# Splitting an expert's weights only where the expert changes, for slots 2 to 4 of a mixture of experts

## The chip, the cores and the metric

The kernel runs on one core of a Trainium2 chip, in one launch. The metric is device time in microseconds; lower is better. A core has five engines that run beside each other and wait for each other by semaphores: TensorE (PE in the profile, its weight loads as PEld), VectorE (DVE), ScalarE (ACT), GpSimd (POOL) and SyncE (SP), which here only issues transfers.

## The reference, cut to what matters

Three layers follow each other; all arrays are float32 (`w_in` and `w_out` are drawn as float32 too, the kernel is handed them as float64 bits).

```python
# 1. attention: 4 batches x 8 heads, 576 tokens, head size 64, with a decay by f, causal
scores = where(causal, -1e9, q @ k.T / 8 + cum[:, None] - cum[None, :]);  x = softmax(scores) @ v
# 2. mixture of experts, one expert per token: 2304 tokens, D = 512, 8 experts, F = 1024
e_idx = argmax(x @ w_gate + modality_bias[modality_id]);  gate = softmax(...)[e_idx]
for e in range(8):
    mask = e_idx == e
    out[mask] = gate[mask] * (relu(x[mask] @ w1[e]) @ w2[e])
# 3. feed-forward: 512 -> 2048 -> 512
h = x @ w_in;  y = maximum(0.01 * h, h) @ w_out
```

## The kernel before, in words

**Precision.** A float32 product is made of three matmuls of a faster 32-bit format: a matrix is split in a high half (a cast, done by ScalarE) and a low half (matrix less high half, by VectorE), and high x high, low x high and high x low are summed in PSUM. Activations and weights are split so, on the chip.

**Attention** (to about 232 us) runs over 16 pairs of heads. Its last pieces overlap with the first of the experts. While it runs, the tokens are routed: `route(b)` per batch finds each token's expert and its place among that expert's tokens. After three of four batches `route1` already lays out the first `K1 = 4` *slots*: a slot is 128 tokens of one expert, and the first slots are filled with the experts' full groups of 128, in the order of the experts. `ef` is the expert of each slot, `nw` is 1 where it differs from the slot before (always 1 for slot 0), `ei` and `ni` are these as integers. `finish` lays out the other slots once all batches are routed; its first part and the rest of `route(3)` are written ahead of the slots' loop, outside of any fixed order, so the planner puts their instructions between others.

**Experts.** `step(t)` runs for each slot: the first 18 always, up to 7 more under nested conditions (`rest`), and `tail` ends it. Step t does slot t's first product and, one step late, slot t-1's second. In the order of TensorE: `gemm1(t)` for k 0 and 1 (12 matmuls of 512 columns), `trh(t-1)` (8 transposes of slot t-1's hidden layer, split in `hh` and `hl`), `gemm1(t)` for k 2 and 3, `gemm2(t-1)` for k 0 to 3, `trx(t+1)` (4 transposes of the next tokens, split in `xh` and `xl`), `gemm2(t-1)` for k 4 to 7; in step 0 and for t < 3 `trh` and `trx` stand a little elsewhere. `keep(t)`, on ScalarE, takes `gemm1`'s result through the relu to `hs`; `yout(t)` scales the second product by the gate and scatters it.

The weights of an expert are 4 + 4 tiles of 128 x 1024. `load(t, which, k)` brings one of them (512 KB) into `w1r[k]` or `w2r[k]`; from slot 1 on the transfer has a condition, a register made from `ni`, and is not carried out where the expert is the same. `split(t, which, k)` then makes `w1h[k]`, `w1l[k]` (or `w2h`, `w2l`) of it with one ScalarE cast and one VectorE subtraction, for every slot, and issues the load of slot t+1 into the tile that has come free. There is one set of raw and of split tiles. `split(t+1, 0, k)` stands in step t, each k where `gemm1(t)` is done with that tile; `split(t, 1, k)` stands in step t, k 0 and 1 behind the first half of `gemm2(t-1)`, k 2 and 3 at the end of the step.

**Order.** `with ordered(tc, MS2)` fixes the order of all five engines as it is written in the steps; what is written outside is placed by a planner that simulates the times. A conditional block (`tc.If`) is a piece of its own: nothing is put between its instructions. Beside the experts, the first weights of the third layer are loaded and converted in small pieces (`wpart`, `aside`). **The third layer** follows from about 499 us on, in the planner's order.

```python
nc.scalar.copy(hi[k], raw[k])
nc.vector.tensor_tensor(lo[k], raw[k], hi[k].bitcast(F32), ALU.subtract)
if t + 1 < NS:
    load(t + 1, which, k)
```

Of the kernel before, what the change touches and what calls it, by code (L numbers as in the profile page):

```python
# [9 lines left out]
F32 = mybir.dt.float32  # L10
F32R = mybir.dt.float32r
BF16 = mybir.dt.bfloat16
I32 = mybir.dt.int32
AF = mybir.ActivationFunctionType
ALU = mybir.AluOpType
AX = mybir.AxisListType
# [3 lines left out]
P = 128  # L20
# [11 lines left out]
NS = NSTAT + E - 1  # L32
# [5 lines left out]
K1 = 4  # L38
# [35 lines left out]
def fused(ctx: ExitStack, tc, qk0, qk2, vp, f, mid, wg, mb, w1, w2, w_in, w_out, out):  # L74
    nc = tc.nc
    w_in = w_in.bitcast(I32)
    w_out = w_out.bitcast(I32)
    cp = ctx.enter_context(tc.tile_pool(name="const", bufs=1))
# [43 lines left out]

    gidx, oidx, ei, ni = ([cp.tile([P, n] + d, I32, name=f"{c}{n}") for n in (K1, N2)] for c, d in (("gidx", []), ("oidx", [2]), ("ei", []), ("ni", [])))
    nt = cp.tile([P, 1], I32, name="nt")

    mr = ExitStack()
    rt = mr.enter_context(tc.tile_pool(name="rt", bufs=1, side="right"))
# [13 lines left out]
    with tc.tile_pool(name="pst", bufs=PST, space=PSUM) as pst:  # L141
# [48 lines left out]
        def load(g):  # L190
            if g == 1:

                xt[0] = pe.tile([P, NC, XW], F32, tag="x", name="x0")
                raw = xt[0].rearrange("p c d -> p (c d)")[:, :2 * S].rearrange("p (h s) -> p h s", h=2)
            else:
                raw = pe.tile([P, 2, S], F32, tag="raw", name=f"raw{g}", bufs=3)
            nc.sync.dma_start(raw, qk2[:, 2 * g:2 * g + 2, :])
            ops[g] = raw
# [234 lines left out]
        def xout(g):  # L433
            b, gg = divmod(g, H // 2)
            if gg == 0 and b:
                xt[b] = (pe, pre)[b % 2].tile([P, NC, XW], F32, tag="x", name=f"x{b}")
            x = xt[b]
            lp = lps[b % 2]
            rr = a3.tile([P, NC, 2], F32, tag="rr", name=f"rr{g}")

            nc.vector.tensor_copy(sms[g % 3][:64, 4, 1:2], sms[g % 3][64:, 4, 0:1])
            nc.vector.tensor_scalar(rr, sms[g % 3], 1e-9, None, ALU.add)
            nc.vector.reciprocal(rr, rr)
            for part, c0, n in ((0, 0, 3), (1, 3, 2)):
                xu = st.pop((g, "x", part))
                ps = pst.tile([P, 512], F32, tag="t", name=f"xo{g}_{part}")
                for i in range(n):
                    nc.tensor.matmul(ps[:, i * HW:(i + 1) * HW], lhsT=xu[:, i * P:(i + 1) * P], rhs=idw[:, gg, :], start=True, stop=True)
                i0 = ps[:, :n * HW].rearrange("p (c d) -> p c d", d=HW)
                sc = rr[:, c0:c0 + n, :].unsqueeze(3)  # L450
                for o, a, w in ((x[:, c0:c0 + n, gg * P:(gg + 1) * P], slice(0, P), D), (lp[:, c0:c0 + n, gg, :], slice(P, HW), E)):
                    nc.vector.tensor_tensor(o.rearrange("p c (j d) -> p c j d", j=2), i0[:, :, a].rearrange("p c (j d) -> p c j d", j=2), sc.to_broadcast([P, n, 2, w]), ALU.mult)
            if gg == H // 2 - 1:
                routing.append(route(b))
                if b == B - 2:
                    routing.append(route1(pre, (B - 1) * NC))
# [77 lines left out]
        def scan(a, n):  # L534
            t = [rt.tile([P, 4 + E], F32, name=f"scan{n}{i}") for i in range(2)]
            for i in t:
                nc.vector.memset(i, 0.0)
            nc.vector.tensor_copy(t[0][:, 4:], a)
            for s in (1, 2, 4):
                nc.vector.tensor_add(t[1][:, 4:], t[0][:, 4:], t[0][:, 4 - s:4 + E - s])  # L540
                t = t[::-1]
            inc = t[0][:, 4:]
            exc = rt.tile([P, E], F32, name=f"exc{n}")
            nc.vector.tensor_sub(exc, inc, a)
            return inc, exc

        def slots(tp, n, inc):
            s3 = [P, n, E]
            gi = tp.tile(s3, F32, name=f"gi{n}")
            nc.vector.tensor_tensor(gi, slott[:, :n].unsqueeze(2).to_broadcast(s3), inc.unsqueeze(1).to_broadcast(s3), ALU.is_ge)  # L550
            ef = rt.tile([P, n], F32, name=f"ef{n}")
            nc.vector.tensor_reduce(ef, gi, axis=AX.X, op=ALU.add)
            return gi, ef

        def per_token(tp, name, a, m):
            s2 = [P, m, E]
            u = tp.tile(s2, F32, tag="u", name=f"u{name}")
            nc.vector.tensor_tensor(u, oall[:, :m], a.unsqueeze(1).to_broadcast(s2), ALU.mult)
            o = tp.tile([P, m], F32, name=name)
            nc.vector.tensor_reduce(o, u, axis=AX.X, op=ALU.add)  # L560
            return o


        def table(tp, n, m, stk, pool, tag, h2p):
            s4 = [P, m, n]
            h1 = tp.tile(s4, BF16, name=f"h1{n}")
            nc.vector.tensor_tensor(h1, slott[:, :n].unsqueeze(1).to_broadcast(s4), stk.unsqueeze(2).to_broadcast(s4), ALU.is_equal)
            h2 = h2p((m, 2, n))
            for i in range(2):
                nc.vector.tensor_tensor(h2[:, :, i, :], h1, idf[:, i, :m].unsqueeze(2).to_broadcast(s4), ALU.mult)  # L570
            yield
            ps = pool.tile([P, 512], F32, tag=tag, name=f"tp{n}")
            for i in range(m):
                r = rows_of(i % NC)
                nc.tensor.matmul(ps[:, :2 * n], lhsT=lall[:r, i, :], rhs=h2[:r, i].rearrange("p a t -> p (a t)"), start=(i == 0), stop=(i == m - 1))
            tq = tp.tile([P, 2 * n], F32, name=f"tq{n}")
            nc.vector.tensor_copy(tq, ps[:, :2 * n])
            idt = rt.tile([P, n], F32, name=f"idt{n}")
            nc.vector.scalar_tensor_tensor(idt, tq[:, :n], 64.0, tq[:, n:], ALU.mult, ALU.add)
            nc.vector.tensor_scalar(gidx[n == N2], idt, -1.0, 0.0, ALU.add, ALU.max)  # L580
            yield idt
# [4 lines left out]
        def route1(tp, m):  # L586
            fi = tp.tile([P, E], I32, name="fi")
            full = rt.tile([P, E], F32, name="full")
            nc.vector.tensor_copy(fi, runb)
            nc.vector.tensor_scalar(fi, fi, 7, None, ALU.logical_shift_right)  # L590
            nc.vector.tensor_copy(full, fi)
            yield
            inc, exc = scan(full, 1)
            yield
            used = rt.tile([P, E], F32, name="used")
            nc.vector.tensor_scalar(used, exc, -1.0, float(K1), ALU.mult, ALU.add)
            nc.vector.tensor_scalar(used, used, 0.0, None, ALU.max)
            nc.vector.tensor_tensor(used, used, full, ALU.min)
            yield
            gi, ef = slots(rt, K1, inc)  # L600
            nw = tp.tile([P, K1], F32, name="nw1")
            nc.vector.memset(nw, 1.0)
            nc.vector.tensor_tensor(nw[:, 1:], ef[:, 1:], ef[:, :K1 - 1], ALU.not_equal)
            nc.vector.tensor_scalar(ei[0], ef, float(E - 1), None, ALU.min)
            nc.vector.tensor_copy(ni[0], nw)
            yield
            stk = per_token(tp, "stk1", exc, m)
            yield
            lim = per_token(tp, "lim1", full, m)
            yield  # L610
            nc.vector.tensor_tensor(lim, jall[:, :m], lim, ALU.is_ge)
            nc.vector.scalar_tensor_tensor(stk, lim, BIG, stk, ALU.mult, ALU.add)
            nc.vector.tensor_add(stk, stk, jall[:, :m])
            yield
            for _ in table(tp, K1, m, stk, pst, "t", lambda d: tp.tile([P, *d], BF16, name="h2")):
                for _ in range(T1):
                    yield
            early.update(full=full, used=used, gi=gi, ef=ef)
# [170 lines left out]
    with tc.tile_pool(name="rt2", reuse_waits="tile", bufs=1) as rt2, \  # L789
# [40 lines left out]
            nc.gpsimd.indirect_dma_start(out=xg[t % 2], out_offset=None, in_=xs[:n, :], in_offset=bass.IndirectOffsetOnAxis(ap=m[:, i:i + 1], axis=0), bounds_check=n - 1, oob_is_err=False)  # L830

        def split(t, which, k):
            raw, hi, lo = (w2r, w2h, w2l) if which else (w1r, w1h, w1l)
            nc.scalar.copy(hi[k], raw[k])  # L834
            nc.vector.tensor_tensor(lo[k], raw[k], hi[k].bitcast(F32), ALU.subtract)  # L835
            if t + 1 < NS:
                load(t + 1, which, k)

        def trx(t):
            ps = pmx.tile([P, 512], F32, tag="tx", name=f"tx{t}")  # L840
# [57 lines left out]
        def tail(t):  # L898
            with ordered(tc, MS4):
                trh(t)  # L900
                ps = [(pmx, "tx"), (pm0, "th"), (pm1, "th")]
                xtr(0, xp0, ps, [0])
                split(t, 1, 2)
                split(t, 1, 3)
                gemm2(t, 0, 4)
                xtr(0, xp0, ps, [1, 2, 3])
                gemm2(t, 4, NFB)
                yout(t)
# [5 lines left out]
        def step(t):  # L914
            nx = t + 1 < NS
            if not t:
                split(t, 1, 0)
                split(t, 1, 1)
# [260 lines left out]
```

## Time and profile before

| | |
|---|---|
| time, median of 3 runs | 914.2 us (913.07 to 915.13) |
| profiled execution, its own time | 911.09 us |
| its span, first to last instruction | 909.4 us |
| TensorE busy | 863.0 us (95%) |
| VectorE busy | 629.2 us (69%) |
| ScalarE busy | 526.4 us (58%) |
| GpSimd busy | 141.9 us (16%) |
| one weight split | 1054 or 1051 ns on ScalarE, 1221 or 1217 on VectorE |
| weight splits | 84 of w1, 80 of w2 (20 slots ran) |

The page also cuts the span in 40 slices of 22.7 us, a digit for the busy tenths of each:

```profile
PE   5999899898979999999999999999999999999995
DVE  6677768588899999999987364368336943473333
ACT  5877767577768899999986353354223422232221
PEclk9999999999999999999999999999999999999998
```

The experts lie in slices 11 to 22. An engine's idle time costs something only where another, in the end TensorE, waits for it; which wait that is, is read from the timeline. PEclk is the clock granted to TensorE.

### The profile page before, as it was taken

How to read it: one execution, taken by the hardware profiler on the slowest of the kernel's cores; microseconds unless marked ns; L12 is line 12 of the kernel's file. 1: busy time of each engine (PE TensorE's matmuls, PEld its weight loads, DVE VectorE, ACT ScalarE, POOL GpSimd, SP SyncE). 2: the span in 40 equal slices, each digit the busy share in tenths (PEclk: the TensorE clock that was granted, in tenths of full speed). 3: DMA queues.
4: the chain of work that ended last, by engine and by line, in shares of the span. 5: the costliest groups of instructions: out<-in, count | busy, mean ns of one | idle time of the engine just before them, and what ended most of it. 6: DMA issues, size and time to landing. Idle time of an engine off the chain costs nothing. (4 is left out here: it accounts for less than half of the span.)

```text
span 909.4 us, 14373 instructions
## 1 busy us (share of the span) xinstructions
PE 863.0 (95%) x4733; PEld 710.0 (78%) x4733; DVE 629.2 (69%) x1091; ACT 526.4 (58%) x993; POOL 141.9 (16%) x181
## 2 busy tenths in 40 slices
PE   5999899898979999999999999999999999999995
PEld 3877777776758788888877888888888888888885
DVE  6677768588899999999987364368336943473333
ACT  5877767577768899999986353354223422232221
POOL 5000000000112324454532100000000000001112
PEclk9999999999999999999999999999999999999998
DMA  5776867758338516422231232024000400011111
GB/s 154 221 175 166 210 162 176 200 120 276 74 98 281 155 42 188 132 70 70 84 103 38 83 94 81 1 70 114 2 1 25 136 27 0 1 47 47 47 47 69
DMA packets 32962, 92.91 MB, mean 102 GB/s; under 512 B 7317, under 2 KB 7989, under 8 KB 32882
## 3 DMA queue, kind: packets, MB, share of 16 engines
q1 hardware_dynamic: 28082, 76.71, 29.6%
q0 software_dynamic: 4800, 15.23, 5.3%
q8 instruction: 39, 0.64, 0.3%
q14 instruction: 41, 0.34, 0.1%
HBM read 132.09 MB, written 14.99 MB: 162 GB/s over the span
## 5 line engine op out<-in xcount | busy, mean ns | idle before, releaser
L1085 DVE SCALAR_TENSOR_TENSOR us<-u,us 128x512 f32<-128x512 f32 (+1 forms) x80 | 51.0, 637 | 126.2 <-ACT us L1084 125.6
L1084 ACT COPY us<-u 128x512 f32<-128x512 f32 (+1 forms) x80 | 43.5, 544 | 162.8 <-PE u L1082 162.7
L1082 PE MATMUL u<-fxl,whii 128*128 128x512 f32 (+1 forms) x320 | 118.1, 369 | 0.0
L1082 PE MATMUL u<-fxh,wloi 128*128 128x512 f32 (+1 forms) x320 | 117.9, 368 | 0.0
L1082 PE MATMUL u<-fxh,whii 128*128 128x512 f32 (+1 forms) x320 | 116.8, 369 | 0.7 <-ACT fxh L740 0.7
L1102 PE MATMUL a<-whio,gh 128*128 128x512 f32 x288 | 112.8, 392 | 0.0
L1102 PE MATMUL a<-wloo,gh 128*128 128x512 f32 x288 | 112.3, 390 | 0.0
L1102 PE MATMUL a<-whio,gl 128*128 128x512 f32 x288 | 106.0, 390 | 0.0
L835 DVE TENSOR_TENSOR w1l<-w1r,w1h 128x1024 fp32r<-128x1024 f32 x84 | 100.8, 1221 | 4.6 <-ACT w1h L834 4.1
L835 DVE TENSOR_TENSOR w2l<-w2r,w2h 128x1024 fp32r<-128x1024 f32 x80 | 94.4, 1217 | 0.9 <-ACT w2h L834 0.7
L834 ACT CAST w1h<-w1r 128x1024 fp32r<-128x1024 f32 x84 | 85.8, 1054 | 2.3 <-PE h L854 2.2
L339 ACT ACTIVATE p<-sc,nm 128x128 f32<-128x128 f32 (+3 forms) x128 | 66.1, 526 | 31.3 <-DVE nm L334 28.4
L834 ACT CAST w2h<-w2r 128x1024 fp32r<-128x1024 f32 x80 | 81.4, 1051 | 2.8 <-PE y L882 2.2
L1088 ACT CAST gh<-us 128x512 fp32r<-128x512 f32 (+1 forms) x80 | 46.2, 578 | 58.7 <-DVE us L1085 39.4
L1089 DVE TENSOR_TENSOR gl<-us,gh 128x512 fp32r<-128x512 f32 (+1 forms) x80 | 50.9, 636 | 39.8 <-ACT gh L1088 39.0
L334 DVE TENSOR_REDUCE nm<-sc 128x2 f32<-128x256 f32 (+1 forms) x64 | 51.1, 819 | 30.0 <-PE sc L328 22.5
L882 PE MATMUL y<-w2h,hl 128*128 128x512 f32 x160 | 64.0, 400 | 5.5 <-DVE hl L875 5.4
L1112 POOL DMA_INDIRECT out<-acc,tid x18 | 17.9, 995 | 327.2 <-DVE acc L1109 290.1
L1082 PEld LDWEIGHTS u<-fxh,whii 128*128 128x128 f32 x320 | 60.2, 188 | 11.1 <-ACT fxh L740 0.9
L1082 PEld LDWEIGHTS u<-fxh,wloi 128*128 128x128 f32 x320 | 60.3, 188 | 10.4
L1082 PEld LDWEIGHTS u<-fxl,whii 128*128 128x128 f32 x320 | 60.3, 188 | 10.2
L882 PE MATMUL y<-w2h,hh 128*128 128x512 f32 x160 | 65.3, 408 | 0.0
(263 smaller groups left out, 1839.4 us busy)
## 6 DMA issues: line engine op xcount, KB each, us to landing
w1r<-w SPq DMA_DIRECT2D x88, 512.0 KB
w2r<-w SPq DMA_DIRECT2D x82, 512.0 KB
rwi<-w_in SPq DMA_DIRECT2D x16, 512.0 KB
rwo<-w_out SPq DMA_DIRECT2D x16, 512.0 KB
raw<-qk SPq DMA_DIRECT2D x14, 576.0 KB
vt<-vp SPq DMA_DIRECT2D x16, 320.0 KB
xr<-yd SPq DMA_DIRECT2D x18, 256.5 KB
bk<-aq SPq DMA_DIRECT2D x15, 288.0 KB
```

What stands on the lines that cost most here:

```text
L334: nc.vector.tensor_reduce(nm, view, axis=AX.X, op=ALU.max, negate=True)
L339: nc.scalar.activation(pt[:, j, :], view[:, j, :], AF.Exp, bias=nm[:, j:j + 1], scale=1.0, accum_out=sms[g % 3][:, c, j:j + 1])
L834: nc.scalar.copy(hi[k], raw[k])
L835: nc.vector.tensor_tensor(lo[k], raw[k], hi[k].bitcast(F32), ALU.subtract)
L882: nc.tensor.matmul(Yp[t], lhsT=ap[:, k * P:(k + 1) * P], rhs=wp[k // 2][:, k % 2, :], start=(k == 0 and i == 0), stop=(k == NFB - 1 and i ...
L1082: nc.tensor.matmul(ps, lhsT=w[:, c], rhs=x[:, k, :], start=(k == 0 and i == 0), stop=(k == NKB - 1 and i == 2))
L1084: nc.scalar.copy(us, ps)
L1085: nc.vector.scalar_tensor_tensor(us, ps, 0.01, us, ALU.mult, ALU.max)
L1088: nc.scalar.copy(gh, us)
L1089: nc.vector.tensor_sub(gl, us, gh.bitcast(F32))
L1102: nc.tensor.matmul(A[b][i], lhsT=x[:, c], rhs=w, start=(first and m == 0), stop=(last and m == 2))
L1112: d = nc.gpsimd.indirect_dma_start(out=out[:, :], out_offset=bass.IndirectOffsetOnAxis(ap=tid[:, c:c + 1], axis=0), in_=Y[b, i], in_offset ...
```

## The change

For slots 1 to 3 (the second to the fourth) and each of the two matrices, the four splits are gathered in one block at the place of the last of them, and the block is executed only where the slot's expert differs from the slot before. The condition is a bit of a word: `nw` times the powers of two in `pw`, summed, is written to `nb` in `route1`; ScalarE and VectorE read it once each into a register, and test bit t. The loads for slot t+1 follow behind the block, all four together. Slot 0 and the slots from 4 on are as before.

```diff
+    nb = cp.tile([P, 1], I32, name="nb")
+    pw = cp.tile([P, K1], F32, name="pw")
+    for t in range(K1):
+        nc.gpsimd.memset(pw[:, t:t + 1], float(2 ** t))
...
             nc.vector.tensor_copy(ni[0], nw)
+            nc.vector.tensor_tensor(nw, nw, pw, ALU.mult)
+            word = tp.tile([P, 1], F32, name="word")
+            nc.vector.tensor_reduce(word, nw, axis=AX.X, op=ALU.add)
+            nc.vector.tensor_copy(nb, word)
...
         def split(t, which, k):
+            if not 0 < t < K1:
+                parts(which, k)
+                if t + 1 < NS:
+                    load(t + 1, which, k)
+            elif k == 3:
+
+                if not WD:
+                    WD.append(nc.values_load(nb[0:1, 0:1], engines=(mybir.EngineType.Activation, mybir.EngineType.DVE), min_val=0, max_val=2 ** K1 - 1))
+                with tc.If(((WD[0] >> t) & 1) != 0):
+                    for i in range(4):
+                        parts(which, i)
+                for i in range(4):
+                    load(t + 1, which, i)
+
+        WD = []
+
+        def parts(which, k):
             raw, hi, lo = (w2r, w2h, w2l) if which else (w1r, w1h, w1l)
             nc.scalar.copy(hi[k], raw[k])
             nc.vector.tensor_tensor(lo[k], raw[k], hi[k].bitcast(F32), ALU.subtract)
-            if t + 1 < NS:
-                load(t + 1, which, k)
```

## Rows read from the trace of the kernel before

**Rows 1.** Stretches: length, busy us (count) of PE PEld DVE ACT POOL; PEclk, DMA, GB/s.

```profile
232.00:246.00 14.00, 14.00 (x76) 11.31 (x75) 13.73 (x29) 9.91 (x14) 1.47 (x1) 1.00 0.20 67
259.00:273.00 14.00, 8.79 (x50) 6.60 (x48) 13.51 (x25) 6.53 (x8) 0.81 (x2) 0.88 0.50 159
```

**Rows 2.** Timeline of TensorE: start, us, what, count [idle before, released by].

```profile
252.79 0.74 PE L854 MATMUL h<-w1h,xl 128*128 128x512 f32 x2 [0.28 <-DVE xl L844]
...
264.71 0.80 PE L882 MATMUL y<-w2h,hl 128*128 128x512 f32 x1 [5.21 <-DVE hl L875]
265.31 0.63 PE L882 MATMUL y<-w2h,hh 128*128 128x512 f32 x1
...
268.00 0.39 PE L882 MATMUL y<-w2l,hh 128*128 128x512 f32 x1
268.23 0.39 PE L882 MATMUL y<-w2h,hl 128*128 128x512 f32 x1
...
313.02 0.73 PE L854 MATMUL h<-w1h,xl 128*128 128x512 f32 x2 [1.13 <-DVE xl L844]
```

**Rows 3.** Groups of VectorE, 232 to 265.2 us: busy us, mean ns, idle before.

```profile
L835 DVE TENSOR_TENSOR w1l<-w1r,w1h 128x1024 fp32r<-128x1024 f32 x9 | 10.8, 1215 | 0.0
L835 DVE TENSOR_TENSOR w2l<-w2r,w2h 128x1024 fp32r<-128x1024 f32 x8 | 9.6, 1213 | 0.0
L875 DVE TENSOR_TENSOR hl<-th,hh 128x512 fp32r<-128x512 f32 x4 | 2.6, 680 | 0.0
```

**Rows 4.** Timeline of VectorE.

```profile
233.69 0.77 DVE L466 TENSOR_REDUCE lgs<-lp 128x40 f32<-128x320 f32 x1
...
261.82 1.10 DVE L570 TENSOR_TENSOR h<-h,idf 128x420 bf16<-128x420 bf16 x2
...
263.98 1.28 DVE L875 TENSOR_TENSOR hl<-th,hh 128x512 fp32r<-128x512 f32 x2
...
294.16 1.23 DVE L835 TENSOR_TENSOR w1l<-w1r,w1h 128x1024 fp32r<-128x1024 f32 x1 [0.28 <-ACT w1h L834]
```

**Rows 5.** Loads of L825: ns min/median/max, first to last; 221 to 264.2, then 266 to 271.

```profile
L825 SPq DMA_DIRECT2D w1r<-w x12: 73/73/101, 222.3 to 252.0; - x12
L825 SPq DMA_DIRECT2D w2r<-w x8: 73/73/87, 236.1 to 264.1; - x8
...
L825 SPq DMA_DIRECT2D w1r<-w x4: 333/336/343, 266.4 to 269.8; - x4
```

**Rows 6.** Timelines of TensorE and ScalarE where slot 0 gives way to slot 1.

```profile
238.22 0.62 PE L854 MATMUL h<-w1l,xh 128*128 128x512 f32 x2
238.68 0.62 PE L854 MATMUL h<-w1h,xh 128*128 128x512 f32 x2
...
239.55 1.03 ACT L859 ACTIVATE hs<-h 128x1024 f32<-128x1024 f32 x1
```

**Rows 7.** Reading a condition (L1048) and branching on it (L1052): ns min/median/max, first to last.

```profile
L1048 ACTq TENSOR_LOAD <-nt x1: 466/466/466, 461.1 to 461.1; - x1
...
L1052 PEldq COMPARE_BRANCH  x4: 65/142/3783, 457.7 to 487.2; - x4
L1052 ACTq COMPARE_BRANCH  x4: 34/44/50, 461.7 to 487.9; - x4
...
L1052 POOLq COMPARE_BRANCH  x4: 34/39/50, 471.9 to 493.4; - x4
```

**Rows 8.** Timelines of SyncE and ScalarE: slot 2's `keep`, slot 4's loads, its first cast.

```profile
259.66 1.03 ACT L859 ACTIVATE hs<-h 128x1024 f32<-128x1024 f32 x1
...
266.42 3.74 SPq L825 DMA_DIRECT2D w1r<-w  x4
...
274.18 1.05 ACT L834 CAST w1h<-w1r 128x1024 fp32r<-128x1024 f32 x1
```

**Rows 9.** Timelines of GpSimd at the start and of VectorE in the early routing.

```profile
0.33 0.10 POOL L1172 MEMSET const-float32-0.0<- 128x1 f32 x1 [0.33 <-issue]
...
209.93 0.17 DVE L605 CAST ni<-nw 128x4 int32<-128x4 f32 x1
```

**Rows 10.** GpSimd's copies to `tid`, L733: ns min/median/max, first to last start.

```profile
L733 POOL COPY tid<-xr x18: 176/184/1296, 469.1 to 557.8; 128x1 int32<-128x1 int32 x18
```

## The prediction, made before the changed kernel was run

> **What bounds the kernel now.** I read the page's slices first: TensorE stands at nine tenths almost everywhere, so time is to be won only where it stands still or runs slowly. Then the busy time by stretch over the expert steps. In 232 to 246 us TensorE fills its 14 us; in 259 to 273 us it is busy for only 8.79 of 14 and its clock is granted at 0.88; VectorE is busy for 13.73 and 13.51 in the two [rows 1]. So at the start of the expert stage VectorE sets the pace. TensorE's timeline shows what that costs: the third matmul of slot 1's second product waits 5.21 us for `hl`, VectorE's low half of the hidden layer, and the matmuls behind it run slowly until 268.00; one wait of 0.28 us for `xl` stands ahead of it, and one of 1.13 us for a later `xl` at 313 us [rows 2].
>
> Why is `hl` late? VectorE runs without a gap from 232 to 265 us. Between the steps' own work the planner has laid the rest of the routing, 58 small instructions from 233.69 to 262.9 with 13.4 us in sum (first and last of them) [rows 4], and in the same stretch it does 17 weight splits of 1.21 us, 20.4 us [rows 3]. Four of those belong to slot 0 and one to slot 3; 12 are slot 1's `w1l` and `w2l` and slot 2's `w1l`. `hl` starts at 263.98, straight behind such a split [rows 4].
>
> **Does the expert change in slots 1 to 3?** The loads tell it. A conditional load that is not carried out issues in 73 ns, a real one in 333. The 12 `w1r` and 8 `w2r` issues for slots 1 to 3 in 221 to 264 us have medians of 73, none over 101; slot 4's `w1r` have 336 [rows 5]. So on these inputs the word holds bit 0 alone and all six blocks are jumped over: 24 casts of 1.05 us on ScalarE and 24 subtractions of 1.21 us on VectorE go.
>
> **Part by part: what goes.** By the time slot 1's `hl` is wanted, 12 subtractions have gone, 12 x 1.21 = 14.5 us of VectorE's queue. `hl` came 5.2 us late, so VectorE has some 9 us in hand and this wait goes whole: 5.21 us. With it goes the slow stretch: eight starts from 264.71 to 268.00 take 3.29 us, at the 0.23 of the next two they take 1.84: 1.45 us. The `xl` wait goes for the same reason, 0.28. Sum 6.94 us [rows 2]. The 1.13 us at 313 us I leave in place: at 294.16 VectorE waits 0.28 us for ScalarE [rows 4], so it has caught up by then, and it falls behind again by work that is not changed (output indices, w_in's split). Behind `hl` nothing else is late: TensorE itself is next.
>
> **What it adds: a new wait at the first boundary.** Slot 1's splits of w1 stood in step 0 each where a tile came free. Now one block stands behind `keep(0)`, and slot 1's first matmul waits until ScalarE and VectorE have passed it. Today slot 1 starts at 238.68 on the heels of slot 0's last pair (238.22 + 0.62 = 238.84). Now `keep`, 1.03 us [rows 6], comes between: some 238.9 to 239.9. Each hand-over between engines costs about 0.05: `hl`'s first half, 263.98 + 0.68 [rows 3, 4], ends 0.05 ahead of TensorE's start at 264.71. So slot 1 starts at about 240.1, 1.4 us later. All of TensorE's work is queued behind that matmul, so the 1.4 count in full. Reading the word (0.47 us on ScalarE's sequencer) and comparing and branching (0.03 to 0.05) [rows 7] run while `keep` executes; without that cover they cost some 0.6, once. VectorE passes its block earlier, behind slot 1's `xl` at 238. Does an idle of 1.3 us slow the clock? After 1.13 us of idle the next pair takes a normal 0.73, after 5.21 us single matmuls took 0.8 and 0.63 [rows 2]; 1.13 is the nearer, so I take no loss, and 1.45 us as the other end. At the other five blocks TensorE has at least the previous slot's second product to do, 24 matmuls at 0.23, 5.5 us, between the block's place and its first reader, so they cost nothing unless they take longer than that.
>
> **What it moves: slot 4's loads.** They are real, and the four of each matrix now issue together behind slot 3's block instead of one by one. For w1 that is behind `keep(2)`, which ends at 260.7 today and would at 262.1; at today's spacing (four in 3.7 us from 266.42) they issue from 262.2 to 266. ScalarE takes the first at 274.18 today, without idle ahead of it [rows 8], and 5.1 us earlier then, at 269.1. That is 6.9 us behind its issue, against 7.8 today. I take 0; the other end is the 1 us of lead lost, and it would hit everything queued behind that cast on ScalarE, slot 2's `hh` first, which TensorE needs. w2's four wait for `yout(2)` and are wanted only behind the next step's first product, so they have as long. On SyncE the loads of slots 2 and 3 stay unexecuted, and w_in's load, which queues behind slot 2's, comes earlier.
>
> **What it adds elsewhere.** Three small VectorE instructions in the early routing, 0.17 us each like the cast ahead of them, stand in front of the maxima that ScalarE waits for [rows 9]: between 0 and 0.5, I take 0.3. Four memsets of one column on GpSimd in the first microseconds, 0.1 us each [rows 9]: between 0 and 0.4, I take 0.1, as most of GpSimd's work there is not waited for.
>
> **Sum.** -6.94 + 1.4 + 0.3 + 0.1 = -5.1 us. The profiled execution took 911.09 us (span 909.4), so 906.0. The median of the runs is 914.2, 3.1 us above that execution; with the same difference the forecast is 909.1 us.
>
> **A rule that speaks against it.** At the end of the step chain the trace has jumps over conditional steps: on ScalarE and GpSimd a branch takes 34 to 50 ns, but TensorE's longest takes 3783 ns [rows 7]. The Trainium skill ("Runtime: NRT & Kernel Launch", Instruction fetch mechanics) says that a taken branch whose target lies outside the two pages of instructions at hand must wait for a DMA to bring them. By the short rows the sum stands; by that rule a block's jump may cost a fetch. TensorE's row agrees with it, where the most instructions are skipped; the others show that a shorter jump need not pay.
>
> **The rivals.** (a) *A jump costs a fetch.* If the first block's jump takes 3.78 us, as TensorE's did, from 239.6 on, slot 1 starts at about 243.6: 3.5 us more, and after 4.9 us of idle the clock is down, 1.45. -5.1 + 3.5 + 1.45 = -0.2: 914.0, no change. At the other blocks 3.8 us lie inside the 5.5. For it: the 3783 ns. Against: four instructions with their waits make a short jump, and the rows of 34 to 50 ns.
>
> (b) *The planner takes a block as a fence* for the instructions that it lays freely. Then the 13.4 us of routing all run ahead of the first block: VectorE starts them at 233.7, has two splits of slot 0 and `xl` to do besides (3.1 us) and passes the block at 250.2. Slot 1 starts 11.6 us late instead of 1.4, with a slow clock: -5.1 + 10.2 + 1.45 = +6.5: 920.7, slower. It decides as soon as more than some 5 us of the routing are put ahead of the block. For it: a block is one indivisible piece, and what was spread between 12 splits needs new places. Against: GpSimd's copies to `tid`, written behind all conditional steps, run from 469.1 on, ahead of its first branch at 471.9 [rows 7, 10]; so free instructions do cross blocks.
>
> (c) *The same mechanism, a smaller gain*: the clock falls at the new wait, or routing that no longer stands between splits crowds ahead of slot 0's `hl`: -5.1 + 1.45 + up to 1, about -3: 911.2.
>
> (d) *The blocks are executed after all.* Then slot 1 waits for `keep` and four splits, some 5 us more, VectorE's queue is as long as before and idles for `keep`; part of that replaces the wait for `hl`: about +2.5, 916.7. Rows 5 speak against it.
>
> (e) *Nothing comes of it*, because ScalarE holds TensorE just as long once VectorE doesn't. It is busy for 9.91 and 6.53 us in the two stretches [rows 1], so I give it little: 914.
>
> **How the numbers follow.** The forecast has 0.58 (its own range 907 to 911), (c) 0.14, (a) and (e) together 0.11, (b) 0.13, (d) 0.04. About 0.2%, 1.8 us, is what a measurement of this kernel can tell from no change. Faster by more than that: the forecast and most of (c), 0.71. Within it: (a), (e) and the edge of (c), 0.12. Slower: (b) and (d), 0.17. The range's lower end is the sum without its costs (-6.9) and a microsecond of scatter, 906.0; the upper end takes in (c), (a) and (e), 914.8.
>
> **What would show it.** Right: no wait of `y` for `hl` near 260 us, full clock from 246 to 300 us, a wait of 1.2 to 1.5 us of `h` behind `keep(0)`, released by ScalarE, slot 4's loads in one bunch, and its first cast without idle ahead of it. Wrong: a branch of microseconds on ScalarE or VectorE; the routing on VectorE in one run ahead of the first block; `w1h` or `w2h` of slot 4 waiting for a load; or other gaps in the attention or in the last 410 us, which should be as they were.

## The result, and the profile after

The changed kernel takes 904.72 us (median of 6 runs, 902.25 to 907.6) against 913.63 of the kernel before in the same session (911.26 to 915.13): ratio 0.9904, 95% interval 0.9879 to 0.9928. Three more sessions gave 0.9908, 0.9922 and 0.9913. The forecast was 909.1 with a range from 906.0: the direction is right, the gain of 8.9 us is larger than the 5.1 foreseen, and the time lies below the range. The profiled execution took 902.25 us (span 900.4).

The stretches after, same columns and bounds as [rows 1]. TensorE is now full where it was busy for 8.79 us, at full clock, and VectorE has room; what TensorE misses lies in the first stretch.

```profile
232.00:246.00 14.00, 13.13 (x69) 10.56 (x68) 12.00 (x44) 5.29 (x9) 1.51 (x1) 1.00 0.43 104
259.00:273.00 14.00, 14.00 (x83) 11.31 (x82) 6.15 (x10) 7.25 (x11) 3.61 (x4) 1.00 0.80 236
```

VectorE's groups from 232 to 265.2 us, as [rows 3]: no `w1l` is left and four `w2l`, all slot 0's. The idle time behind the bar is new.

```profile
L861 DVE TENSOR_TENSOR w2l<-w2r,w2h 128x1024 fp32r<-128x1024 f32 x4 | 4.9, 1218 | 0.0
L899 DVE TENSOR_TENSOR hl<-th,hh 128x512 fp32r<-128x512 f32 x4 | 2.6, 683 | 2.9 <-ACT hh L898 2.9
L868 DVE TENSOR_TENSOR xl<-tx,xh 128x512 fp32r<-128x512 f32 x3 | 2.1, 687 | 5.1 <-ACT xh L867 5.1
```

TensorE's waits over the whole span (what waited, for what; us in total, times, longest). The wait for `hl` of 5.21 us [rows 2] is gone, 0.2 in sum is left of that kind, and in the expert stage there is one new row, ScalarE's queue at the block (L850).

```profile
PE h L878 <- DVE xl L868: 2.1, 2, 1.1
PE th L896 <- DVEq L1076: 1.9, 1, 1.9
...
PE h L878 <- ACTq L850: 0.9, 1, 0.9
...
PE y L906 <- DVE hl L899: 0.2, 1, 0.2
```

The first boundary, TensorE's timeline. Slot 0's last pair gives way at 237.40, slot 1 starts at 238.79, 1.39 us later; in between run the seven routing matmuls (`rk`) that stood behind slot 1's first twelve before.

```profile
236.93 0.63 PE L878 MATMUL h<-w1l,xh 128*128 128x512 f32 x2
237.40 0.19 PE L494 MATMUL rk<-oall,before 128*128 128x32 bf16 x1
...
237.66 0.26 PE L499 MATMUL rk<-oall,onesb 128*128 128x40 bf16 x4
238.79 0.73 PE L878 MATMUL h<-w1h,xh 128*128 128x512 f32 x2 [0.87 <-ACTq L850]
```

ScalarE there, its timeline: `keep(0)` (L883), then the block, then slot 0's casts of `w2`.

```profile
237.60 1.02 ACT L883 ACTIVATE hs<-h 128x1024 f32<-128x1024 f32 x1 [2.08 <-PE h L878]
238.81 2.00 ACT L860 CAST w2h<-w2r 128x1024 fp32r<-128x1024 f32 x2 [0.19 <-ACTq L850]
```

Reading the word (L849) and the six blocks' branches (L850), ns min/median/max, first and last start. None is longer than 72 ns, and over the whole span VectorE does 72 splits for `w1l` and 68 for `w2l`, where it did 84 and 80: all six blocks are jumped over, and no jump takes microseconds.

```profile
L849 ACTq TENSOR_LOAD <-nb x1: 466/466/466, 237.6 to 237.6; - x1
L849 DVEq TENSOR_LOAD <-nb x1: 816/816/816, 238.0 to 238.0; - x1
...
L850 ACTq COMPARE_BRANCH  x6: 45/45/55, 238.5 to 277.9; - x6
...
L850 DVEq COMPARE_BRANCH  x6: 56/56/72, 239.0 to 275.8; - x6
```

Slot 4's loads of w1 on SyncE and their first cast on ScalarE, which had been idle ahead of it for TensorE and not for the load: issue to cast is 7.2 us, 7.8 in [rows 8].

```profile
259.05 2.68 SPq L834 DMA_DIRECT2D w1r<-w  x4
```

```profile
266.26 1.05 ACT L860 CAST w1h<-w1r 128x1024 fp32r<-128x1024 f32 x1 [1.25 <-PE h L878]
```

Not foreseen is the clock elsewhere. In 222 to 228 us, at a stand-still of 2.3 us at the end of the attention that both kernels have, the execution before was granted 0.72 and the one after full clock (columns as rows 1).

```profile
222.00:228.00 6.00, 4.77 (x25) 4.01 (x27) 5.53 (x11) 5.00 (x12) 0.00 (x0) 0.72 0.48 187
```

```profile
222.00:228.00 6.00, 5.04 (x33) 3.08 (x33) 4.61 (x10) 5.46 (x13) 0.00 (x0) 1.00 0.26 97
```

The mean granted clock was 0.987 before and 0.995 in this execution.

### The profile page after: what moved, and what is told of

Same layout as the page of the kernel before. It is cut to its first block, busy times and chain, and to the rows that moved or that the text cites. A ratio compares the mean times of both kernels' runs of the same rounds, so it can differ in the third digit from the quotient of the medians.

```text
span 900.4 us, 14345 instructions
## 1 busy us (share of the span) xinstructions
PE 855.9 (95%) x4733; PEld 703.2 (78%) x4733; DVE 602.7 (67%) x1070; ACT 504.9 (56%) x969; POOL 121.4 (13%) x185
## 5 line engine op out<-in xcount | busy, mean ns | idle before, releaser
L861 DVE TENSOR_TENSOR w1l<-w1r,w1h 128x1024 fp32r<-128x1024 f32 x72 | 86.4, 1220 | 10.3 <-ACT w1h L860 10.0
L861 DVE TENSOR_TENSOR w2l<-w2r,w2h 128x1024 fp32r<-128x1024 f32 x68 | 80.2, 1218 | 0.7 <-ACT w2h L860 0.6
L860 ACT CAST w1h<-w1r 128x1024 fp32r<-128x1024 f32 x72 | 73.6, 1053 | 3.7 <-PE h L878 3.7
L860 ACT CAST w2h<-w2r 128x1024 fp32r<-128x1024 f32 x68 | 69.4, 1051 | 3.5 <-PE y L906 2.2
L1126 PEld LDWEIGHTS a<-whio,gl 128*128 128x128 f32 x288 | 54.1, 188 | 11.5
```

The costliest lines, as they stand in the source:

```text
L1126: nc.tensor.matmul(A[b][i], lhsT=x[:, c], rhs=w, start=(first and m == 0), stop=(last and m == 2))
```

## The experiments

**How times are compared.** The granted clock differs from execution to execution, and takes the time with it. So beside the ratio stands d, the difference in microseconds to the kernel before at equal mean clock: one straight line through all 293 runs of this study (7.3 us per 0.01 of clock), a constant for each kernel, with its 95% interval. The kernel before has 117 runs, median 913.53, mean clock .9866.

| kernel | median us (runs) | ratio, 95% interval | clock | d |
|---|---|---|---|---|
| the change, four times | 904.66 (26) | .9904, .9908, .9922, .9913 | .9905 | -5.7 ± 0.5 |
| e1_static | 904.02 (6) | .990 [.9869, .993] | .9907 | -6.4 ± 0.9 |
| e5_static_w1 | 907.31 (6) | .9936 [.9915, .9958] | .9893 | -4.8 ± 0.9 |
| e6_static_w2 | 907.76 (12) | .9941 [.9922, .996] | .9905 | -3.0 ± 0.7 |
| e3_gather | 916.37 (12) | 1.0033 [1.0017, 1.0049] | .9908 | +5.6 ± 0.7 |
| e4_early | 904.65 (6) | .9908 [.9881, .9936] | .9913 | -5.4 ± 1.0 |
| e11_early2, e18_early3 | 906.65 (6), 904.09 (6) | .9916, .9901 | .9905 | -5.4 ± 0.7 |
| e2, e12, e14: the word alone | 911.16, 911.61, 912.69 (12 each) | .9971, .998, .9999 | .9903, .9883, .9873 | -0.3 ± 0.4 |
| e9_memsets | 914.68 (12) | .9999 [.9977, 1.002] | .9857 | 0.0 ± 0.7 |
| e10_dve, e16_dve2 | 914.82, 913.33 (12 each) | .9999, 1.0003 | .9863 | -0.1 ± 0.5 |
| e7_placebo, e15_placebo2 | 914.05, 912.93 (12 each) | 1.0011, 1.0004 | .9860 | -0.1 ± 0.5 |

**The wait without the block, and the other parts alone.** `e1_static` writes the program without the splits of slots 1 to 3; it has neither word nor block, and its loads stay where they were. It is right for these inputs alone.

```diff
-            nc.scalar.copy(hi[k], raw[k])
-            nc.vector.tensor_tensor(lo[k], raw[k], hi[k].bitcast(F32), ALU.subtract)
+            if not 0 < t < K1:
+                nc.scalar.copy(hi[k], raw[k])
+                nc.vector.tensor_tensor(lo[k], raw[k], hi[k].bitcast(F32), ALU.subtract)
```

> The kernel before, with the splits of slots 1 to 3 left out when the program is written (right for these inputs, on which the expert doesn't change there); no word, no blocks, the loads where they were. Theory Q (VectorE's queue was the bound, the new wait behind keep(0) costs 1.4 us): no idle of y for hl, no wait behind keep(0), so 1.2 to 1.8 us faster than the change: some 10.3 us under the kernel before (about 903). Rival F (blocks and moved loads cost nothing, the wait behind keep(0) is covered elsewhere): same as the change within 0.5 us (904.7). Rival A (most of what exceeded the forecast comes from the attention, through the three new routing instructions or the memsets and the order that the planner then finds): 2 us or more slower than the change (907 or more), as the attention is the old one here.

It has the whole gain without any of the change's machinery, and neither the wait for `hl` nor one at the boundary. So the gain comes from the splits that are not done; block, word and moved loads together cost 0.7 of d, within the error of the two and less than the 1.2 to 1.8 us expected. By TensorE's starts, from slot 0's last pair to 300 us, it is 1.0 us.

`e2_word` computes the word and uses it nowhere:

```diff
+            if True:
+                parts(which, k)
+                if t + 1 < NS:
+                    load(t + 1, which, k)
```

> The change without its effect: the word is computed (memsets, three VectorE instructions) but never read, and all splits and loads are as before. Theory Q: within 0.5 us of the kernel before, 0 to 0.4 us slower; the 5.2 us idle for hl is there. Rival A: 1.3 to 3 us faster than the kernel before.

Its profile has the wait for `hl` as before (5.2 us), and d is +0.2 ± 0.7; the ratio of .9971 is clock, of which more below.

`e3_gather` has the change's places (four splits at once behind `keep`, loads behind them) and executes them always:

```diff
-                with tc.If(((WD[0] >> t) & 1) != 0):
-                    for i in range(4):
-                        parts(which, i)
+                for i in range(4):
+                    parts(which, i)
```

> The four splits of slots 1 to 3 gathered at the place of the last and always executed, loads moved behind them, no condition. Theory Q: slot 1's first matmul waits for keep(0) and the four splits, some 5 to 6 us of idle at 239 us, VectorE's queue is as long as before, part of the wait for hl is replaced: 1.5 to 4 us slower than before. Rival: VectorE's queue alone sets the end of this stretch, and a gathered order only changes where TensorE waits: within 1 us of before.

It is slower than before, as expected, but the wait at 239 us is 1.69 us and not 5 to 6. Its TensorE timeline from 238 to 300 us, the waits alone: what were waits of 0.28 and 5.21 us are seven, 8.84 us in sum. The gathering only loses; rival (d) would have looked much like this, with the loss spread over later waits.

```profile
239.84 0.73 PE L875 MATMUL h<-w1h,xh 128*128 128x512 f32 x2 [1.69 <-ACT w1h L857]
...
248.76 0.50 PE L903 MATMUL y<-w2h,hl 128*128 128x512 f32 x1 [1.39 <-DVE hl L896]
...
256.17 0.73 PE L875 MATMUL h<-w1h,xl 128*128 128x512 f32 x2 [1.17 <-DVE xl L865]
...
264.41 0.50 PE L903 MATMUL y<-w2h,hl 128*128 128x512 f32 x1 [1.56 <-DVE hl L896]
...
283.01 0.66 PE L863 MATMUL tx<-ident,xg 128*128 128x128 f32 x4 [1.50 <-DMA xg<-xs,gidx]
```

**How many splits the wait hangs on.** `e6_static_w2` leaves out w2's splits of slots 1 to 3 alone (four of the twelve ahead of `hl`), `e5_static_w1` w1's alone (eight).

```diff
+            if not which or not 0 < t < K1:     # e6;  in e5: if which or not 0 < t < K1:
                 nc.scalar.copy(hi[k], raw[k])
                 nc.vector.tensor_tensor(lo[k], raw[k], hi[k].bitcast(F32), ALU.subtract)
```

> The kernel before with only the w2 splits of slots 1 to 3 left out when the program is written. Theory Q by amount: ahead of slot 1's hl, 4 subtractions of 1.21 us go, 4.9 us of the 5.2 us by which it is late; 0.2 to 0.8 us of that wait is left, and with so short a wait no fall of the clock behind it: 5.5 to 6.5 us faster than before at equal other falls. Rival (the wait is for something else that VectorE only passes on): the wait keeps over 2 us.

> The kernel before with only the w1 splits of slots 1 to 3 left out. Theory Q by amount: 8 subtractions go ahead of slot 1's hl, 9.7 us, more than it is late: the wait is gone whole, as with all of them left out, within 0.5 us of that run at equal clock. Rival: part of it stays, since routing instructions take the freed places.

With four gone, 4 x 1.21 = 4.9 us less in VectorE's queue, 0.81 of the 5.21 us is left (timeline of e6); with eight gone nothing near 260 us is left. That is VectorE's queue, split by split. No run leaves out the subtractions without the casts; that VectorE's half decides is read from rows, from `hl` straight behind a split [rows 4] and ScalarE busy for 9.91 and 6.53 of 14 us [rows 1].

```profile
251.71 0.74 PE L855 MATMUL h<-w1h,xl 128*128 128x512 f32 x2 [0.28 <-DVE xl L845]
...
259.23 0.50 PE L883 MATMUL y<-w2h,hl 128*128 128x512 f32 x1 [0.81 <-DVE hl L876]
```

In d, e5 is 1.6 us behind e1, where 0.5 at most was expected. TensorE's rows show where most of that went: it waits 0.41 us for a gather of tokens at 274.49, and at the conditional steps, outside of what was changed, longer than in e1 (e5, then e1); in e6 that wait is 3.02 us. Why is open.

```profile
482.11 1.97 PE L873 MATMUL th<-ident,hs 128*128 128x128 f32 x8 [2.78 <-ACTq L1053]
```

```profile
480.67 1.06 PE L873 MATMUL th<-ident,hs 128*128 128x128 f32 x8 [1.95 <-DVEq L1053]
```

**Can the new wait be had back?** `e4_early` puts the block ahead of `keep(t)`:

```diff
+            if t + 1 < K1:
+                split(t + 1, 0, 3)
...
-            if nx:
+            if nx and t + 1 >= K1:
```

> The change, with the block of the next slot's w1 ahead of keep(t) instead of behind it for slots 1 to 3. Theory Q: the idle of 0.87 us behind keep(0) goes and slot 1 starts 1.0 to 1.4 us earlier: 1.0 to 1.4 us faster than the change (about 903.5). Rival: VectorE's pass of the block (its register read took 0.82 us) ends the wait just as late: within 0.3 us of the change.

The wait at the boundary is gone, and another of the same size is there (its timeline): the last tables of the routing got ahead of slot 2's `xl` on VectorE.

```profile
251.81 0.73 PE L878 MATMUL h<-w1h,xl 128*128 128x512 f32 x2 [1.05 <-DVE xl L868]
```

`e11_early2` also moves that part of the routing back, into step 1 and behind slot 2's `xl` (`next(tb)` now stands behind the first `yield` and not ahead of it).

> The block of the next slot's w1 ahead of keep(t), and besides the last three large instructions of the routing's first part (the table, 1.7 us) moved into step 1, behind xl of slot 2, which they delayed by 1.05 us in the run with the block ahead of keep alone. Theory Q: neither the idle of 0.87 us behind keep(0) nor the 1.05 us is there: 1.0 to 1.5 us faster than the change at equal clock, about 903.5. Rival: VectorE's routing delays something else (hl of slot 1, or the table's matmuls at step 3): the same as the change within 0.5 us.

Now neither wait is there: TensorE's next one is 0.16 us at 299.17 in the second run of this version, which stood beside the change on one chip:

> The version with the early block and the routing's table part moved, now beside the change on one chip. If the wait at the first boundary costs what TensorE's starts say (1.0 us net of the routing matmuls that run in it), it is 0.5 to 1.5 us faster than the change; if what it frees is lost again in the attention (TensorE came out of it 3 us later in that version's first profile), within 0.5 us of the change or slower.

> The change again, as the measure for the version beside it: 8 to 9.5 us less than the kernel before, clock .003 to .005 above it.

From slot 0's last pair to that `y`, by TensorE's starts, it is 1.1 us less than in the change. The medians, 904.09 and 904.56, point the same way but don't resolve it, and by d the version is not ahead: not shown to be faster.

**Where the clock's part comes from.** After the first runs the word alone had shown a clock of .9903 with the wait for `hl` still in place. So its parts were run alone, beside a comment as the measure of nothing.

```diff
+    pw = cp.tile([P, K1], F32, name="pw")          # e9: these alone
+    for t in range(K1):
+        nc.gpsimd.memset(pw[:, t:t + 1], float(2 ** t))
...
+            nc.vector.tensor_tensor(nw, nw, slott[:, :K1], ALU.mult)   # e10, e16: these alone
+            word = tp.tile([P, 1], F32, name="word")
+            nc.vector.tensor_reduce(word, nw, axis=AX.X, op=ALU.add)
+            nc.vector.tensor_copy(nb, word)
```

> The kernel before with only the tile pw and its four memsets on GpSimd. Theory P1 (the memsets at the start, or the addresses that move with the tile, shift the attention against its transfers, and fewer stand-stills end in a fall of the clock): clock 0.990, 1.5 to 2.5 us faster than before. Theory P2 (the three routing instructions do it): 0.987, the same within 0.7 us.

> The kernel before with the tile nb and the three VectorE instructions of the word (by another constant, no memsets), unread. Theory P2: clock 0.990, 1.5 to 2.5 us faster than before. Theory P1: 0.987, within 0.7 us of before, or up to 0.5 us slower by VectorE's time.

> The kernel before with nothing changed but a comment. The runs so far list, for the kernel before, a mean granted clock of 0.987 (23 runs) and for all changed kernels 0.990 to 0.992, that of the word alone too: about two half-speed stretches of 3.4 us fewer, some 1.4 us each. Theory C (chance of a build or of the order of runs): this copy has some 0.990 too and is 1 to 2.5 us faster than the kernel before. Theory P (the program's own timing decides whether a stand-still ends in a fall): 0.987 and the same time within 0.7 us.

> The word alone, computed and not read, once more, with the change on the same chip. Its memsets and its three instructions left the mean granted clock at 0.986 each by itself (another chip than the word's first runs, which had 0.990 against 0.987). Theory P (the whole word's program shifts the stand-stills so that fewer end in a fall): 0.990 again, some 2 us faster than before. Theory C (chance of that chip or load): 0.986, within 0.7 us of before.

> The change once more. Theory Q with P: 8 to 9 us faster than before, mean clock 0.991. With C: the shift at equal clock, some 5.3 us, and 1.4 us for the fall at hl that is always gone: 6 to 7 us faster, mean clock 0.988 to 0.989.

The parts and the comment did nothing (d of 0.0 to 0.2, clock .9851 to .9859), the word again had more clock than before (.9883), and the change beside it .9910, but on another chip than the parts. The last session of this kind had all on one chip:

> The word is computed and not read, all splits as before; run on one chip beside the comment, the word's VectorE part and the change. Theory P (the word's presence by itself lowers the number of half-speed stretches): mean granted clock at least .003 above the kernel before and the comment, time 2 to 3 us less. Theory C (the number of stretches differs by chance of the execution and chip, and falls lastingly only where the wait for hl goes): clock within .0015 of the comment's, time within 1.5 us of it.

> The kernel before with a comment at its end, as the measure of what no change gives. Both theories: within 1 us of the kernel before, clock within .001 of it.

> The three VectorE instructions of the word without the four memsets (the multiplier is another table of the routing). Theory P, if VectorE's part is what matters: clock .003 above the comment's, 2 to 3 us less; if the memsets matter, as the comment. Theory C: as the comment, within 1.5 us and .0015 of clock.

> The change again. Both theories: 8 to 10 us less than before, clock .004 to .005 above it. By P the word has some .003 of that clock and is to show it in its own run; by C the whole of it belongs to the wait that is gone, and the word's own run shows none.

There the word alone has .9873 (standard error .0007), the comment .9870, the VectorE part .9867, the change .9898. So the word doesn't lift the clock on that chip; why it ran at .9903 and .9883 on the other one stays open. What separates the kernels is the wait. In each of the nine profiles with the full wait for `hl` the clock falls to half at it: in five for one stretch as in [rows 1, 2], in four for twice as long, as here (e12, columns as rows 1, and its timeline). None of the eleven profiles without the full wait has one between 230 and 480 us.

```profile
257.00:271.00 14.00, 8.79 (x34) 6.77 (x33) 13.73 (x45) 5.77 (x7) 2.28 (x3) 0.76 0.30 91
```

```profile
266.50 0.79 PE L906 MATMUL y<-w2h,hl 128*128 128x512 f32 x1 [5.21 <-DVE hl L899]
...
270.08 0.63 PE L906 MATMUL y<-w2l,hh 128*128 128x512 f32 x1
...
270.91 0.60 PE L866 MATMUL tx<-ident,xg 128*128 128x128 f32 x4
```

The other falls, at stand-stills of 1.5 to 4.2 us near 113, 167, 223 and 485 us that every kernel here has (the end apart), come and go: 27 stretches in the nine profiles with the wait, 30 in the eleven without (3.0 and 2.7 in a profile). That the profile of the change showed one of them alone, in 167 us, was luck of that execution.

## Why the prediction was wrong in size and right in kind

**The mechanism holds.** VectorE's queue of splits made `hl` late, and the wait goes with them; the loads told truly that no expert changes in slots 1 to 3. `e13_after2` shows it best, as its profile has the clock's falls at 114, 170, 224 and 484 us, like the execution before (its attention took 0.73 us longer, the first offset below). Its TensorE rows:

```profile
238.49 0.62 PE L878 MATMUL h<-w1h,xl 128*128 128x512 f32 x2
...
240.80 0.50 PE L878 MATMUL h<-w1h,xh 128*128 128x512 f32 x1 [0.87 <-ACTq L850]
...
253.79 0.62 PE L878 MATMUL h<-w1h,xl 128*128 128x512 f32 x2
...
260.23 0.40 PE L906 MATMUL y<-w2h,hl 128*128 128x512 f32 x1
...
262.06 0.39 PE L906 MATMUL y<-w2l,hh 128*128 128x512 f32 x1
```

The same matmuls before start at 237.76 (a row of that timeline), 238.68, 252.79, 264.71 and 268.00 [rows 2, 6]. The offset goes +0.73, +2.12, +1.00, -4.48, -5.94. Term by term:

| term | predicted | measured |
|---|---|---|
| new wait behind `keep(0)` | +1.4 | +1.39 |
| from there to slot 2's `xl` | -0.28 | -1.12 |
| wait for `hl` | -5.21 | -5.48 |
| half-speed matmuls behind it | -1.45 | -1.46 |
| three VectorE instructions, memsets | +0.4 | 0 by themselves (d of e9, e10, e16: 0.0 ± 0.7, -0.1 ± 0.5) |
| sum | -5.1 | -6.7 |

**The step that failed: the waits that go were priced by the idle in brackets.** The prediction took 5.21 and 0.28 us as what these waits cost. A bracket counts from the end of the matmul ahead, 0.39 us long, while in a row the matmuls start 0.23 apart [rows 2]: 0.16 us of each wait lies outside of it. And the first two matmuls behind a wait start 0.34 us apart (246.26 and 246.60 below), 0.11 more. So the wait for `xl` cost 0.54 us and not 0.28, and one that was missed, where slot 0's `hl` is first used, has no bracket and cost 0.35. It shows in the starts, before (0.47 and 0.34 us apart) and in e13 (0.24 and 0.23):

```profile
245.79 0.39 PE L882 MATMUL y<-w2l,hh 128*128 128x512 f32 x1
246.26 0.50 PE L882 MATMUL y<-w2h,hl 128*128 128x512 f32 x1
246.60 0.40 PE L882 MATMUL y<-w2h,hh 128*128 128x512 f32 x1
```

```profile
247.60 0.40 PE L906 MATMUL y<-w2l,hh 128*128 128x512 f32 x1
247.84 0.39 PE L906 MATMUL y<-w2h,hl 128*128 128x512 f32 x1
248.07 0.39 PE L906 MATMUL y<-w2h,hh 128*128 128x512 f32 x1
```

Of the 0.84 us more up to slot 2's `xl`, 0.35 come there and 0.15 at `xl`; 0.27 are the `rk` matmuls, which now run inside the new wait (the offset falls there from 2.12 to 1.85); the rest is spread. The 0.27 more at `hl` are the pair behind `xl` and what the bracket of 5.21 leaves out. With the 0.4 of cost that doesn't show here, this is 1.5 us.

**A cost that was not foreseen.** Behind the stage some of it is lost again: TensorE's work from 320 to 485 us takes 0.46 to 0.48 us longer in the change's four profiles than in the one before. So it does in all seven others of programs that compute the whole word, read or not (0.44 to 0.48), and in none of the other nine, e9 and e10 among them (-0.12 to 0.11 from the kernel before). Most of it lies in `y`'s matmuls of `w2l` and `hh`, which start 232.5 ns behind those ahead of them instead of 227.6. Why is open.

**And the clock's term was mis-sized.** The prediction took the one fall that the profiled execution showed, 1.45 us, as the price of the wait. Over all runs the change has .0039 more clock, 2.8 us by the line of 7.3 per 0.01; d carries the other 5.7. By the profiles the fall at `hl` is 13 stretches in nine, 1.44 in the mean: some 1.9 us, as five of nine cost 1.45 to 1.6 and a double one costs 2.1 (e12: ten starts from 266.50 to 270.91 take 4.4 us, at 0.23 each 2.3; e14 alike) to 2.9 (e2, e16). The 0.9 us that remain have no place: the mean number of the other falls is too uncertain to say whether they became rarer.

**The account.** Forecast to result: -5.1, then -1.5 in the stage, +0.5 behind it and -1.4 of clock make -7.5. The difference of the means over all runs is -8.6, that of the medians in the first session -8.9; some 1.1 to 1.4 us stay without a place in the rows. The base adds to the miss: the forecast stood on 914.2, the median of three runs, and the session of the result had 913.63. The range's lower end, by the prediction's own words 914.2 - 6.9 - 1 = 906.3, was written as 906.0; all four medians of the change, 904.56 to 904.94, lie below either.

**The costs held.** The new wait is 1.39 us for 1.4. In none of the change's four profiles did the clock fall at it, and slot 0's `hl` came without a delay (e13 at 247.84, above), so rival (c) is out. VectorE reads the word in 0.82 us, where I had 0.47 for ScalarE alone [rows 7], and comes out of its block at 239.38, not at 238 (its timeline, below); TensorE first reads `w1l` some 1.0 us behind its start at 238.79, as two pairs stand ahead, so this cost nothing, by less than half a microsecond. No row shows a cost of the loads in a bunch: no cast of slot 4 waits for one.

```profile
237.96 0.21 DVE L502 COPY rks<-rk 128x48 f32<-128x48 f32 x1 [0.58 <-PE rk L499]
239.38 0.20 DVE L504 TENSOR_TENSOR ps<-rks,runb 128x40 f32<-128x40 f32 x1 [1.21 <-DVEq L850]
```

**The rivals.** (a) is refuted: 45 to 72 ns a branch. The Trainium skill ("Runtime: NRT & Kernel Launch", Instruction fetch mechanics) says that a taken branch waits for a fetch where its target lies outside the instructions at hand. The trace doesn't contradict it, as these jumps pass over four casts or four subtractions with their waits. What a far target costs ScalarE is not separated here: its branches at the conditional steps, one of them over all the steps that are left, are recorded with 50 ns at most [rows 7]. (b) is refuted: VectorE does a part of the routing ahead of the first block (`rks` at 237.96) and the rest behind it (`ps` from 239.38), so the block is no fence for them. In e4 the order did turn against `xl`, for 1.05 us: the rival was real in kind, at a tenth of its price. (d) is refuted by the split counts and by e3, (e) by the result.

## What to carry to other kernels

Price a wait of TensorE by the starts around it, against the same matmuls where nothing waits, and not by the bracket alone: here a wait behind full-speed matmuls cost 0.27 us more than its bracket, and one had none. Where another engine's queue is full, look for more of them. The long wait cost its length and some 1.9 us of slow clock in the mean of nine profiles, where the one at hand showed 1.45; take such a price from several, and compare small changes at equal clock. A condition that both engines read once and test by bit cost 1.4 us at the one boundary where nothing lay between the block and its first reader, most of it for `keep(0)` (1.02), which stands ahead of the block on ScalarE, and no wait of TensorE at the other five.

## What was not expected of the hardware

- The granted clock fell, or did not, at stand-stills of the same length: near 223 us the change stood still for 2.29 and 2.30 us in two profiles, with full clock behind it in the first (1.00 from 222 to 228 us) and half speed for a while in the second, e13 (0.72). The idle's length alone did not decide.
- The same register read of one word took 466 ns on ScalarE and 816 on VectorE; the read of `nt` in the kernel before (L1048) took 466 and 543.
- A kernel with a comment more gave .9988 to 1.0034 in its first session and .9985 to 1.0022 in its second: from one session 0.2 to 0.3% can't be told from nothing here.
